# Block attention with a gated feed-forward: q and k loads of the first batch on one queue, k in whole-head pieces, and a new order of all steps

## The chip, the cores and the metric

One core of a Trainium2 chip runs the kernel. The metric is the device time of one execution in microseconds (us); less is better. The kernel before takes 654.4 us (median of 3 runs, 654.33 to 655.25).

The core's engines run side by side, each with an instruction stream of its own, and wait for one another by semaphores: TensorE (PE, matmuls; its weight loads are listed as PEld), VectorE (DVE), ScalarE (ACT), GpSimd (POOL) and SyncE (SP, which here only issues DMAs). ScalarE and GpSimd can issue DMAs too.

## The reference, cut to what matters

```python
# q, k, v: (4, 8, 768, 64); block = 32, window = 16
k_sum = k.reshape(B, H, nb, block, D).max(axis=3)      # one key per block of 32
v_sum = v.reshape(B, H, nb, block, D).mean(axis=3)     # one value per block
scores_l = where(|i - j| < window, q @ k.T / 8, -1e9)
scores_s = q @ k_sum.T / 8 + log(block)
a = softmax(concat([scores_l, scores_s]))               # with + 1e-9 under the sum
x = (a @ concat([v, v_sum])).transpose(0, 2, 1, 3).reshape(3072, 512)
h = x @ w_in                                            # 512 x 2048
g = h - tanh(h)
return g @ w_out                                        # 2048 x 512
```

All numbers are float32. The program computes its matmuls with operands split in a high and a low part, which is why names such as wh and wl, gh and gl come in pairs.

## The kernel before

The 3072 tokens are eight units u of 384 (two to a batch of 768 tokens), the eight heads two groups g of four, a unit three tiles i of 128 tokens, the 2048 columns of the feed-forward sixteen tiles f of 128. For each unit and group the kernel makes the scores of the 384 queries against 96 local and 24 block keys (`scores`), the softmax in four steps (minimum with the mask on VectorE, exp on ScalarE, the sum's inverse on VectorE, the multiplication called "normal" on any engine), the transposes of the probabilities ("p turn" on TensorE, "p out" back to SBUF), and the values (`values`, out of the tile o). Then come the two matmuls of the feed-forward: "in" (pH), the gate, and "out" (pY). The weights go through `convert`: a load of 512 KB into one of three wraw buffers, then the steps scale, shift, low, sign, which split them into their high and low parts.

q and k need a transposition before they can be used: `load_half` (L809) brings 384 tokens of four heads as four pieces of 96 KB, one for each head, and a "q turn" or "k turn", one instruction of VectorE, that transposes them once all four have landed. `top` (L826) then takes the maximum over each block of k, and "top put" copies it beside the keys. For the first half of the program's work the pieces have buffers in the tiles wg0, wg1 and wg4 (`raw_slots`, L797: six halves); all others ("lazy", L799) go through a single buffer, raw, so that the next four pieces can't be written before the turn of the last four has read it. `load_v` (L847) and `put_mean` (L858) fill the tile vw from v and from the block means with pieces that SP or GpSimd may issue.

Nothing here is issued where the code makes it. `do`, `either` and `dma` record each step as a task with the engines that can run it, what it reads and what it writes, and `Plan.follow` (L150) issues all tasks afterwards. The order of the tasks is a list of 3628 numbers written out in the source, `ORDER` (L29); `ON` (L33) has a letter for each task, which names the engine where there is a choice (P, A, D, S for GpSimd, ScalarE, VectorE, SyncE); `FILL` (L32) says ahead of which tasks TensorE runs keep-warm matmuls whose results nobody reads, and how many: long ones of 512 columns until the scores, short ones of 128 after them. Within an engine the instructions run in the order of that list; a task that waits holds up what is behind it on its engine. The planner's costs (the rates in `dma`, L463) serve for plans without a list. All instructions show the line L58, the wrapper that issues them, so rows are told apart by tile names: wg<-in_k and wg<-in_q are the first batch's q and k pieces, raw<-in_k and raw<-in_q the lazy ones, kT<-wg, qT<-raw and oo<-raw the turns, prob, stat and probT the softmax, mean the block means, vw<-in_v and vw<-mean the pieces for the values.

SP's list begins with the four v pieces of group 0, then k, q and v pieces mixed. The first seven entries of ScalarE's list are five k pieces and two q pieces of the first batch, which it issues as DMAs (`both=b == 0` in `load_half` allows that). GpSimd makes the constants (the identity, the mask, zeros), then issues seven v pieces and three mean puts.

## Time and profile before

| what | value |
|---|---|
| median of 3 runs | 654.4 us (654.33 to 655.25) |
| the profiled execution | 654.0 us |
| its span, first to last instruction | 652.3 us |
| TensorE busy | 628.0 us (96%) |
| VectorE busy | 447.1 us (69%) |
| ScalarE busy | 451.2 us (69%) |
| GpSimd busy | 163.3 us (25%) |
| moved by DMA | 113.23 MB |
| mean granted clock of TensorE | 0.996 |

The page comes from one execution. Busy time is the time in which an engine executes; DMA issues and waits are not in it. The stretches (windows) give the same by time, the waits say what an engine's idle time ended with, the chain of waits follows what ended last in a stretch back through what released it, and the timeline lists one engine's instructions. The granted clock is the share of the full speed (1.00 is 2.4 GHz) at which TensorE was allowed to run.

### The profile page before, as it was taken

What the parts mean: (1) busy time and instruction counts of PE and PEld (TensorE: products, weight loads), DVE (VectorE), ACT (ScalarE), POOL (GpSimd) and SP (SyncE); (2) the same over time, 40 slices, a digit from 0 to 9 for tenths busy, and PEclk for the clock granted to TensorE, in tenths of its full rate; (3) what the DMA queues carried; (4) which work ended last, traced back from release to release, by engine and by line L of the source; (5) the groups of instructions that cost most, each with busy time, mean ns of one, the idle gap of its engine ahead of it and who ended that gap; (6) DMA issues with size and microseconds to landing.
All of it is one profiled execution on the core that took longest, in us unless ns stands there. A gap on an engine that the chain in (4) does not pass through costs nothing.

```text
span 652.3 us, 15013 instructions
## 1 busy us (share of the span) xinstructions
PE 628.0 (96%) x5221; PEld 522.9 (80%) x5221; DVE 447.1 (69%) x1271; ACT 451.2 (69%) x1372; POOL 163.3 (25%) x263
## 2 busy tenths in 40 slices
PE   5799899999999999999999999999999999999997
PEld 2464566678888799989888899989888899999885
DVE  3899999996988774555677875645687863333563
ACT  3879798988889755547699865556589754334783
POOL 2302300124202332434533313114311221112120
PEclk9999989999999999999999999999999999999999
DMA  9777787765677586756353356656623145554101
GB/s 237 196 235 224 235 242 227 208 201 167 232 245 261 183 257 210 252 164 213 112 157 116 92 163 218 206 165 198 184 72 95 34 166 190 161 177 148 48 1 51
DMA packets 119340, 113.23 MB, mean 174 GB/s; under 512 B 43561, under 2 KB 87017, under 8 KB 119261
## 3 DMA queue, kind: packets, MB, share of 16 engines
q1 hardware_dynamic: 116716, 109.84, 54.6%
q10 hardware_dynamic: 2176, 1.87, 1.0%
q8 instruction: 42, 0.69, 0.4%
q0 software_dynamic: 368, 0.53, 0.3%
q14 instruction: 38, 0.30, 0.1%
HBM read 88.87 MB, written 20.97 MB: 168 GB/s over the span
## 4 chain that ended last, share of the span: by engine, by line
PE 72%; DMA 12%; DVE 7%; ACT 4%; SPq 2%; issue 2%; POOL 1%; DVEq 0%; ACTq 0%; POOLq 0%
PE pY L58 34%; PE pH L58 26%; PE pS L58 6%; PE pX L58 5%; SPq L58 2%; DVE tmp L58 2%; DMA wraw<-scr 2%; ACT prob L58 2%; DMA raw<-in_q_dram 2%; DMA wraw<-in_moe_w_out_dram 2%; DMA scr<-wraw 1%; DMA raw<-in_k_dram 1%; DMA tmp<-in_v_dram 1%; DVE wf L58 1%; DMA gu<-in_v_dram 1%
## 5 line engine op out<-in xcount | busy, mean ns | idle before, releaser
L58 ACT ACTIVATE prob<-prob,stat 128x120 f32<-128x120 f32 x299 | 109.0, 386 | 17.7 <-DVE stat L58 17.5
L58 PE MATMUL pY<-wl,gh 128*128 128x512 f32 x288 | 113.5, 394 | 0.0
L58 PE MATMUL pH<-wf,wraw 128*128 128x384 f32 x460 | 93.8, 339 | 0.8 <-DMA wraw<-scr 0.8
L58 PEld LDWEIGHTS pH<-wf,wraw 128*128 128x128 f32 x460 | 80.9, 188 | 4.1 <-DVE wf L58 0.9
L58 PE MATMUL pY<-wh,gh 128*128 128x512 f32 x204 | 83.1, 407 | 0.1
L58 PE MATMUL pY<-wh,gl 128*128 128x512 f32 x204 | 81.0, 397 | 0.0
L58 PE MATMUL pH<-wg,wraw 128*128 128x384 f32 x360 | 71.1, 338 | 0.0
L58 PE MATMUL pY<-wg,gh 128*128 128x512 f32 x168 | 68.6, 408 | 0.9 <-ACT gh L58 0.9
L58 ACT ACTIVATE gu<-gu 128x384 f32<-128x384 f32 x128 | 66.2, 520 | 2.1
L58 PE MATMUL pH<-o,wf 128*128 128x384 f32 x188 | 65.8, 446 | 1.6 <-DVE o L58 0.7
L58 POOL TENSOR_TENSOR gl<-gu,gh 128x384 fp32r<-128x384 f32 x32 | 34.0, 1064 | 129.4 <-ACT gh L58 77.5
L58 PE MATMUL pY<-wg,gl 128*128 128x512 f32 x168 | 66.1, 394 | 0.1
L58 PEld LDWEIGHTS pH<-wg,wraw 128*128 128x128 f32 x360 | 63.2, 188 | 3.4 <-issue 0.8
L58 PEld LDWEIGHTS pY<-wl,gh 128*128 128x128 f32 x288 | 54.4, 189 | 9.0
L58 PEld LDWEIGHTS pH<-o,wf 128*128 128x128 f32 x188 | 34.3, 190 | 17.9 <-DVE wf L58 1.5
L58 ACT ACTIVATE gv<-pH 128x384 f32<-128x384 f32 x35 | 17.2, 491 | 42.5 <-PE pH L58 42.5
L58 POOL TENSOR_TENSOR gu<-gu,gt 128x384 f32<-128x384 f32 x26 | 27.1, 1046 | 75.1 <-ACT gu L58 74.3
L58 PEld LDWEIGHTS pY<-wh,gl 128*128 128x128 f32 x204 | 38.6, 189 | 8.8 <-DVE gl L58 0.4
L58 PEld LDWEIGHTS pY<-wh,gh 128*128 128x128 f32 x204 | 38.6, 189 | 7.8 <-issue 0.6
L58 PE MATMUL pY<-wf,gh 128*128 128x512 f32 x108 | 44.8, 440 | 0.0
L58 ACT ACTIVATE gt<-gu 128x384 f32<-128x384 f32 x48 | 24.7, 518 | 22.8 <-DVE gu L58 21.2
L58 PEld LDWEIGHTS pY<-wg,gl 128*128 128x128 f32 x168 | 31.5, 188 | 7.4 <-DVE gl L58 0.5
(232 smaller groups left out, 1420.4 us busy)
## 6 DMA issues: line engine op xcount, KB each, us to landing
wraw<-scr SPq DMA_DIRECT2D x72, 512.0 KB
wraw<-in_moe_w_in_dram SPq DMA_DIRECT2D x16, 512.0 KB
wraw<-in_moe_w_out_dram SPq DMA_DIRECT2D x16, 512.0 KB
scr<-wraw SPq DMA_DIRECT2D x16, 512.0 KB
wraw<-scr SPq DMA_DIRECT2D x24, 256.0 KB
raw<-in_q_dram SPq DMA_DIRECT2D x56, 96.0 KB
vw<-in_v_dram SPq DMA_DIRECT2D x59, 80.0 KB
raw<-in_k_dram SPq DMA_DIRECT2D x48, 96.0 KB
```

The lines of the kernel that those rows point to most:

```text
L58: return lambda *args, **kwargs: self._tc.keep_in_program_order(op(*args, **kwargs))
```

## The change

It has four parts.

- `load_half` loses its `both`: no q or k piece may be issued by ScalarE. The seven pieces go to SP.
- The first batch's k is loaded by a new function, `load_whole`, once for each head group: four pieces of 192 KB, each with both halves of one head, into wg0 and wg4, and two k turns that each wait for all four. q keeps its halves, in wg1. There are eight tasks fewer.
- `ORDER`, `ON` and `FILL` are new from end to end (3620 tasks). SP begins with v, k, v, v, v, k, k, k, then the four q pieces of group 0, then the rest. GpSimd issues twelve v pieces and two mean puts, the first of them right behind its constants; the memset of the zeros beside group 1's keys stands behind ten of these, of which the fourth is a mean put. The mean put that ran on GpSimd as its seventh DMA is on SP. TensorE's list has values matmuls of unit 0 earlier among the first "in" matmuls, the p turns of unit 1, group 1 in another order with the "in" matmuls of the same unit directly behind them, and ahead of the "out" matmuls. Of the tasks with a choice VectorE has ten more than before, ScalarE eight fewer and GpSimd three fewer. FILL has three long matmuls ahead of three tasks as before, and four and three short ones where it had one, two, two and two.
- Two numbers change that have no effect on the issued program: the rate 270e3 (the planner's start times, which a list of the right length overrides), and the 36 in a branch for units listed in `OUT7`, which is empty.

```diff
-ORDER = [1, 6, 13, 14, 27, 15, 16, 117, 0, 9, 28, 30, 10, 17, 24, 19, 18, 20, 22, 29, 48, 46, 25, 47,
...
+ORDER = [15, 17, 16, 1, 9, 6, 2, 3, 10, 13, 14, 109, 4, 19, 110, 18, 20, 111, 23, 24, 25, 42, 41, 44,
...
-FILL = {125: 3, 154: 3, 190: 3, 188: 1, 215: 2, 262: 2, 286: 2}
+FILL = {117: 3, 146: 3, 182: 3, 180: 4, 278: 3}
-ON = 'PPAPAPPDDPPPPSSSSASSADASSADASAADDPSSSS
...
+ON = 'PPAPAPPDDPPPPSSSSSSSSDDSSSSDDASPSSPSPSPPP
...
-            kind, (0.04, 270e3) if run < 1024 else (0.0, 330e3))
+            kind, (0.04, 250e3) if run < 1024 else (0.0, 330e3))
...
-    raw_slots = [(tag, n) for tag in ("wg0", "wg1", "wg4") for n in range(2)]
+    raw_slots, raw_wholes = [("wg1", n) for n in range(2)], ["wg0", "wg4"]
...
-            dma(which + " load", lambda e, h=h, src=src: e.dma_start(x()[32 * h:32 * h + 32].rearrange("p j r d -> p j (r d)"), src), 32 * JH * 2 * D * 4, 2 * D * 4, w=[(base, (n, h))], both=b == 0)
+            dma(which + " load", lambda e, h=h, src=src: e.dma_start(x()[32 * h:32 * h + 32].rearrange("p j r d -> p j (r d)"), src), 32 * JH * 2 * D * 4, 2 * D * 4, w=[(base, (n, h))])
...
+    def load_whole(b, g):
+
+        to, tag = qk_base(b, g)[1], raw_wholes.pop(0)
+        base = buf(("raws", tag), tag, [P, 2, JH, 2, D])
+        for h in (0, 2, 1, 3):
+            src = k[b, HG * g + h].rearrange("(j b r) d -> b j (r d)", j=2 * JH, r=2)
+            dma("k load", lambda e, h=h, src=src: e.dma_start(at(base)[32 * h:32 * h + 32].rearrange("p a j r d -> p (a j) (r d)"), src), 64 * JH * 2 * D * 4, 2 * D * 4, w=[(base, h)])
+        for j in range(2):
+            do("k turn", DVE, TURN_COST, lambda j=j: turn("k", at(base)[:, j], at(to), j), r=[(base, h) for h in range(HG)], w=[(to, j)])
...
     for g in range(NG):
-        load_half("k", 0, g, 0, False)
+        load_whole(0, g)
         load_half("q", 0, g, 0, False)
-        load_half("k", 0, g, 1, False)
         top(0, g)
...
-            if small_only and OUT7 and j >= 36 and (j - 36) % 3 == 0 and (j - 36) // 3 < FH:
-                make_out_sums((j - 36) // 3)
+            if small_only and OUT7 and j >= 66 and (j - 66) % 3 == 0 and (j - 66) // 3 < FH:
+                make_out_sums((j - 66) // 3)
```

## Rows read from the trace of the kernel before

**Rows 1.** The page: TensorE's busy time, and GpSimd's DMA queue (packets, MB, share).

```profile
PE 628.0 (96%) x5221; PEld 522.9 (80%) x5221; DVE 447.1 (69%) x1271; ACT 451.2 (69%) x1372; POOL 163.3 (25%) x263
...
q0 software_dynamic: 368, 0.53, 0.3%
```

**Rows 2.** Stretches: time, busy us (instructions) per engine, granted clock, DMA share, GB/s.

```profile
0.00:16.00 16.00, 8.14 (x110) 4.34 (x116) 4.78 (x6) 4.76 (x20) 4.19 (x22) 1.00 0.94 234
16.00:38.00 22.00, 17.26 (x286) 11.07 (x287) 18.47 (x79) 17.97 (x74) 6.42 (x18) 1.00 0.76 200
...
72.00:88.00 16.00, 12.96 (x134) 8.78 (x133) 14.75 (x49) 13.59 (x48) 5.70 (x5) 0.89 0.86 251
88.00:131.00 43.00, 42.49 (x359) 28.77 (x358) 40.68 (x108) 39.52 (x116) 3.40 (x4) 1.00 0.74 220
...
164.00:252.00 88.00, 85.68 (x781) 73.69 (x782) 72.28 (x204) 65.37 (x196) 20.29 (x28) 1.00 0.72 238
252.00:612.00 360.00, 359.79 (x2775) 320.67 (x2774) 217.01 (x632) 228.19 (x687) 100.36 (x154) 1.00 0.49 153
```

**Rows 3.** What TensorE waited for: us in total, times, longest.

```profile
PE pS L58 <- ACT prob L58: 2.6, 3, 1.3
...
PE pH L58 <- DVE oo L58: 1.5, 1, 1.5
PE pH L58 <- POOL mask L58: 1.4, 1, 1.4
PE pS L58 <- DMA vw<-mean: 0.8, 1, 0.8
```

**Rows 4.** A shorter stretch of the same table, 83.9 to 87.3 us.

```profile
83.90:87.30 3.40, 3.40 (x10) 2.63 (x9) 2.65 (x13) 2.57 (x11) 0.00 (x0) 0.50 0.97 270
```

**Rows 5.** The chain of waits, 0 to 45 us: start, duration, what.

```profile
11.35 2.60 DMA wg<-in_q_dram
...
24.06 0.22 ACT mean L58
...
25.93 4.74 DMA vw<-mean
```

**Rows 6.** The table of stretches again, 11 to 15 us.

```profile
11.00:15.00 4.00, 3.17 (x52) 1.25 (x50) 3.78 (x5) 1.32 (x7) 0.07 (x1) 1.00 1.02 256
```

**Rows 7.** ScalarE's timeline at the start: start, duration, instruction, idle time before.

```profile
7.36 1.28 ACT L58 ACT_TABLE_LOAD   x1 [7.36 <-DMA wg<-in_k_dram]
```

**Rows 8.** GpSimd's timeline, 0 to 45 us: its first DMA issue.

```profile
16.96 0.72 POOL L58 DMA_DIRECT2D vw<-in_v_dram  x1
```

**Rows 9.** VectorE's timeline, 15 to 45 us.

```profile
21.49 0.98 DVE L58 STREAM_TRANSPOSE wg<-wg 128x768 f32<-128x768 f32 x1 [0.73 <-POOL wg L58]
...
31.68 0.56 DVE L58 COPY o<-pS 128x384 f32<-128x384 f32 x1 [0.87 <-PE pS L58]
```

**Rows 10.** The chain of waits, 40 to 92 us.

```profile
46.41 4.66 DMA raw<-in_k_dram
...
72.54 3.82 DMA wraw<-in_moe_w_in_dram
...
76.45 0.68 ACT tmp L58
77.13 1.75 ACT prob L58 x9
...
81.93 0.52 ACT wh L58
```

**Rows 11.** VectorE's timeline, 41 to 92 us.

```profile
45.43 1.25 DVE L58 CAST wh<-wf 128x512 fp32r<-128x512 f32 x1
...
53.84 0.28 DVE L58 TENSOR_SCALAR prob<-prob,stat 128x120 f32<-128x120 f32 x1
...
73.35 0.98 DVE L58 STREAM_TRANSPOSE oo<-raw 128x768 f32<-128x768 f32 x1
```

**Rows 12.** TensorE's timeline, 71 to 92 us: two waits on ScalarE's probabilities.

```profile
81.13 0.61 PE L58 MATMUL pS<-ident,prob 128*120 128x128 f32 x2 [0.25 <-ACT prob L58]
83.08 0.65 PE L58 MATMUL pS<-ident,prob 128*120 128x128 f32 x4 [1.34 <-ACT prob L58]
```

4 lines of the change are left out of this document (2 added, 2 removed).

## The prediction

> **What bounds the kernel now.** Three views, in this order: the page's busy shares, the table of stretches, and TensorE's waits; then the chain of waits in the two stretches where TensorE is not full. The page says that TensorE is busy 628.0 of 652.3 us [rows 1]: whatever else the change does, at most 24 us can be won from outside the matmuls, and the matmul count does not change. The stretches say where the 24 us lie [rows 2]: 7.9 us in the first 16 us, 4.7 in 16 to 38, 3.0 in 72 to 88, 0.5 in 88 to 131, 2.3 in 164 to 252, next to nothing in the 360 us behind that, and 4.6 at the very end (the last store, which the change doesn't reach). So the change is decided in the first 90 us, and the question behind that is how much of a gain is given back between 88 and 252 us, where VectorE is busy 40.68 of 43 us and ScalarE 39.52 [rows 2].
>
> The waits name the releasers [rows 3]: ScalarE's probabilities 2.6 us in three waits (the longest 1.3), one wait of 1.5 on VectorE's oo (the q turn ahead of the scores of unit 1, group 1), 1.4 on POOL's mask (the first scores), 0.8 on the block means that a DMA brings back. Beside the waits stands one loss that no wait shows: from 83.9 to 87.3 us the granted clock is 0.50, the lower level (1.2 of 2.4 GHz) [rows 4]; what ran in those 3.4 us would have taken 1.7 at the upper level. It follows the waits on ScalarE's probabilities.
>
> The time against which I add is the profiled run: 654.0 us, span 652.3, so 1.7 us outside the span. The median is 654.4, 0.4 above; I add 0.4 at the end.
>
> **The start (0 to 16 us).** Before the first scores the same v, k and q bytes have to land, in the old and in the new order; 8 of the k issues become 4 of double size. In the trace the last q piece lands 2.60 us after its issue, at 13.95 [rows 5]; behind it come the q turn on VectorE, the top copy and the mask on POOL, and the scores. Meanwhile the DMA engines move 256 GB/s at a mean share of 1.02 [rows 6]: the start is bound by bytes, not by issues. Five k pieces and two q pieces leave ScalarE's queue, which starts its table load only at 7.36, behind them [rows 7]; ScalarE has no other work then that anyone waits for, so I give its earlier start nothing. SP takes over those pieces, but with the double size it issues 16 k and q pieces there, where it had 17 of the 24: no more issue time than before. What I can't read is the new load of POOL's queue: 12 v pieces and two mean puts issued, by their place in the new order, from about 6 us on, where the old kernel issues its first at 16.96 [rows 8] and 10 in all, with 0.53 MB, or 53 KB each [rows 1]. At 0.72 us an issue [rows 8], at most some six of them, 0.32 MB, could be under way before the q pieces land: 0.32 MB at 256 GB/s are 1.25 us of delay. For a gain speaks that k is there in fewer pieces, that top, turn and mask no longer queue behind each other (TensorE waits 1.4 us for the mask [rows 3]). I take -0.4 us, bounds -1.2 and +1.3.
>
> The Trainium skill ("DMA: Bandwidth & Descriptors", section "Issuing engines are not separate DMA queues") says that transfers started from SP, ScalarE or GpSimd all run on the same 16 engines, so that another issuing queue saves sequencer time alone. The trace agrees as far as it goes: with two queues issuing, the share is full and the rate no higher than later with one. By that rule dropping ScalarE's queue costs nothing, as taken above. The same page ("Queues, rings and completion order") says that an engine serves its queue rows in turn, packet by packet; no run here shows it yet, and it speaks against this change: POOL's early pieces would then not wait behind SP's. That is the third rival.
>
> **16 to 45 us.** The mean put that released the first values matmuls was issued by POOL at 25.93 and landed 4.74 us later [rows 5]; it now stands on SP with 5.67 instead of 5.93 MB of transfers ahead of it (counted in the two orders), some 1 us sooner (gain up to the 0.8 of its wait). VectorE's stall of 0.73 us on a memset of POOL [rows 9] moves: the memset now stands behind ten of POOL's issues, of which the fourth waits for a block mean (about 12 us, as on SP before), so at 12 + 7 x 0.72 = 17 us, still ahead of its reader. Against that, VectorE gets 1.4 us more to do ahead of the turn that starts the lazy q and k loads (softmax normals that ScalarE and POOL had, two block means), and loses the 0.56 us copy of o that it took at 31.68 [rows 9]. The keep-warm matmuls are nine long and seven short in both; the short ones move to where TensorE waits anyway, and cost nothing as long as the wait behind them is longer than the 0.9 us of four. I take -0.3, bounds -1.6 and +1.4.
>
> **The raw chain (45 to 74 us).** The lazy pieces of q and k share one buffer, so each set of four waits for the turn of the set before: the first k set lands 4.66 us after its last issue at 46.41 [rows 10]. Ahead of the first k pieces a weight load waited for VectorE; in the new order three of four k pieces stand before that load, and the weight step it waits for comes about 1 us sooner behind the turn. Over the whole stretch up to the last q turn (73.35 [rows 11]), VectorE loses the copy of o (0.56), one cast of 1.25, and five normals of 0.28, and gets seven normals and two block means of about 0.22 (ScalarE's time for the same step [rows 5]; VectorE has no such row, bounds 0.1 and 0.4); the other moves (a probT copy, a weight scale) cancel. Net 1.25 + 0.56 - 2 x 0.28 - 2 x 0.22 = 0.8 us less [rows 11]. So the turn comes at about 71 to 72, TensorE arrives 0.7 us earlier, and of its wait of 1.5 us I take 1.2 away; bounds -1.5 and +0.8 (the turn 1.4 later by VectorE's extra work in front, without the gain on the load).
>
> **The softmax behind it (76 to 88 us).** Old: a weight step of 0.68 whose load landed at 76.36 stands ahead of nine exps on ScalarE, and a cast of 0.52 (81.93) between the normals that release the transposes [rows 10]. New: that weight load is issued about 3 us sooner, the five normals on ScalarE stand together and a sixth is VectorE's, so the transposes come 0.6 + 0.7 us sooner. TensorE's waits there are 0.25 + 1.34 us [rows 12]; I take 1.2 away, bounds -1.6 and 0. With no such wait ahead of it I expect the granted clock to stay: -1.4 of the 1.7, bounds -1.7 and 0.
>
> **What is late next.** The sum so far is -0.4 - 0.3 - 1.2 - 1.2 - 1.4 = -4.5 us. TensorE then reaches 88 us 4.5 us sooner, but VectorE was busy 14.75 of the 16 us before and has only 2.3 us free in 88 to 131 [rows 2], and in the new assignment it has 1.5 us more to do up to about 165 and still 1.4 more up to 236, while ScalarE has some 3 us less. Part of what TensorE gains it will wait for VectorE. From below nothing (TensorE's work there is unchanged, its waits 0.5 us), from above 4.4, where VectorE paces it throughout; I take +1.7, nearer to the row of 88 to 131, in which TensorE hardly waits. Behind 252 us TensorE is full and nothing moves.
>
> Sum: 652.3 - 4.5 + 1.7 = 649.5 of span, 651.2 with the 1.7 outside, 651.6 against the median: I say 651.5.
>
> **Rivals.**
> 1. VectorE becomes the bound in 88 to 252 us: the same gains, and 4.0 to 4.4 of them given back. 654.4 - 4.5 + 4.2 = 654.1. For it: 95% busy there [rows 2] and ten more tasks; against it: TensorE's waits in that stretch name VectorE for little of the old 2.3 us.
> 2. The gains in the start and the raw chain come, but the softmax behind the scores ends no sooner, since nine exps and the normals are ScalarE's whatever stands between: 1.2 + 1.4 stay lost, and little is given back (+0.7). 654.4 - 1.9 + 0.7 = 653.2, a faster time within 0.2% of the old.
> 3. Slower: POOL's early v pieces take their share from SP's k and q. It decides from the point where the first q turn starts later than 14.8 + 0.4. Price: 1.25 us at the first scores, which everything behind inherits, and the raw chain starts 1.4 us later by VectorE's extra work ahead of it, so the wait at 73 us grows by 0.8 and the low clock stays; 654.4 + 1.25 + 0.8 = 656.5. For it: the share of 1.02 [rows 6]; against it: the fourth of those issues waits for a mean, so perhaps only three (0.16 MB, 0.6 us) come before the q pieces.
> 4. That the change does not do what it says (k in larger pieces, and no ScalarE issue, moving nothing, the rest of the order a draw): 654.4, a case within the first rival's band.
>
> **How the numbers follow.** About 0.2% (1.3 us) is what a measurement of this kernel can tell from no change. Forecast 0.5 (648.5 to 653.0), rival 1 with 4 0.22, rival 2 0.13, rival 3 0.15. Faster by over 1.3 us: the forecast and most of rival 2's lower edge, 0.57; within: rivals 1, 4, and the rest of 2, 0.25; slower: rival 3 and a little for low clocks that I can't place, 0.18. The range: 648.5 at the low end (the terms at -6.0 and nothing lost more), 656.5 at the high end, at rival 3's price, so that about 0.12 is left out.
>
> **What would show it.** Right: no ScalarE issue before its table load, which starts near 1 us; first scores at 15 to 16 us; the q turn at 71 to 72 and no wait of TensorE over 0.5 us there; transposes without the 1.34 us wait, and a granted clock of 1.00 throughout 72 to 98. Wrong: first scores later than 16.5; a new wait of TensorE on VectorE (wf, probT, gl) in 88 to 252; a second stretch at the 0.50 clock; POOL's issues still the last to land before the first values.

## The result: slower, and the profile after

The changed kernel takes 657.85 us (median of ten runs, 655.32 to 660.37), the kernel before 652.83 beside it (ten runs, 649.99 to 655.25): a ratio of 1.0078 [1.0052, 1.0103]. Run again in a later series it gave 1.0090 [1.0066, 1.0114]. So it is slower by 5 to 6 us, where 651.5 and a gain were predicted, and it lies above the range.

The two profiled executions don't show these 5 us. The changed kernel's took 655.73 us (span 654.0) and is among its fastest; that of before took 654.0 and is among its slower ones. They differ by 1.7 us, and single executions of one kernel differ by up to 5. So the traces are read for what happens, and sizes are taken from repeated runs.

The page of after: TensorE's busy time, which answers [rows 1], and GpSimd's queue.

```profile
PE 627.5 (96%) x5221; PEld 522.1 (80%) x5221; DVE 448.8 (69%) x1281; ACT 448.9 (69%) x1369; POOL 168.2 (26%) x260
...
q0 software_dynamic: 544, 0.79, 0.5%
```

The stretches of after, with the columns of [rows 2]; the last two are the stretch of [rows 4] and a new one.

```profile
0.00:16.00 16.00, 8.29 (x120) 4.40 (x127) 4.86 (x6) 5.19 (x19) 9.12 (x34) 1.00 0.95 221
16.00:38.00 22.00, 18.75 (x286) 10.93 (x270) 19.81 (x82) 16.83 (x71) 3.21 (x8) 0.92 0.84 209
38.00:72.00 34.00, 31.62 (x325) 18.70 (x323) 31.94 (x79) 27.77 (x85) 6.92 (x8) 1.00 0.78 230
72.00:88.00 16.00, 13.60 (x136) 8.31 (x137) 15.45 (x47) 13.87 (x47) 4.42 (x5) 1.00 0.82 243
...
252.00:612.00 360.00, 359.17 (x2773) 319.99 (x2772) 213.64 (x632) 223.96 (x680) 108.62 (x153) 1.00 0.50 153
...
24.20:27.40 3.20, 3.20 (x6) 1.39 (x5) 3.20 (x8) 3.15 (x14) 0.65 (x1) 0.50 0.63 147
83.90:87.30 3.40, 2.81 (x11) 1.80 (x11) 3.32 (x17) 2.80 (x10) 0.00 (x0) 1.00 0.90 255
```

The lower clock has left the place where it stood, 83.9 to 87.3 us, and there is a stretch of 0.50 at 24.2 to 27.4 instead; the last section of the experiments shows that both come and go between executions. What TensorE waited for in after (us in total, times, longest), beside [rows 3]:

```profile
PE pS L58 <- DVE prob L58: 2.1, 1, 2.1
PE pH L58 <- DVE oo L58: 1.6, 1, 1.6
...
PE pH L58 <- DVE qT L58: 1.4, 1, 1.4
...
PE pS L58 <- ACT prob L58: 0.9, 1, 0.9
```

The waits on ScalarE's prob have fallen from 2.6 to 0.9 us. The first scores no longer wait for the mask, but just as long, 1.4 us, for the q turn (qT; in before 0.5). The wait on oo has grown by 0.1 where it should have shrunk by 1.2, and one of 2.1 on VectorE's prob is new. It ends at 22.2 us, and the clock falls behind it. TensorE's timeline of before, 17 to 31 us (start, duration, instruction, idle time before it and what ended it):

```profile
21.30 0.90 PE L58 MATMUL pS<-ident,prob 128*120 128x128 f32 x4 [1.03 <-ACT prob L58]
23.03 0.41 PE L58 MATMUL pS<-ident,prob 128*120 128x128 f32 x2 [0.84 <-ACT probT L58]
23.28 2.74 PE L58 MATMUL pY<-ident 128*128 128x512 f32 x6
```

The same three of after:

```profile
22.20 0.93 PE L58 MATMUL pS<-ident,prob 128*120 128x128 f32 x4 [2.09 <-DVE prob L58]
23.88 0.57 PE L58 MATMUL pS<-ident,prob 128*120 128x128 f32 x2 [0.75 <-DVE stat L58]
24.24 4.34 PE L58 MATMUL pY<-ident 128*128 128x512 f32 x6
```

Six long keep-warm matmuls take 4.34 us instead of 2.74. Part of the delay of prob goes back to VectorE's timeline of after, 14 to 18 us, where the minima with the mask stand behind the second q turn:

```profile
14.35 0.99 DVE L58 STREAM_TRANSPOSE qT<-wg 128x768 f32<-128x768 f32 x1
17.04 0.98 DVE L58 STREAM_TRANSPOSE oo<-wg 128x768 f32<-128x768 f32 x1 [1.70 <-DMA wg<-in_q_dram]
```

The first q turn starts at 14.35 (before 14.79), the second at 17.04, after 1.70 us in which VectorE waited for its last q piece; in before it started at 15.68, right behind the first. The four pieces for it were issued from 10.84 us in after and from 10.25 in before: the issue is 0.6 later, the turn 1.4. The pieces ahead of these do not stand as the section on the change has them: by the trace SP issues three q pieces, three v pieces, the fourth q piece at 9.48 us and one more v piece before them.

The first of the minima in before, where VectorE had been waiting for the scores:

```profile
17.59 0.28 DVE L58 CUSTOM_DVE_ANT_0 prob<-pH,mask 128x120 f32<-128x120 f32 x1 [0.97 <-PE pS L58]
```

and in after, with the weight step behind them:

```profile
18.05 0.28 DVE L58 CUSTOM_DVE_ANT_0 prob<-pH,mask 128x120 f32<-128x120 f32 x1
...
19.65 0.43 DVE L58 TENSOR_SCALAR tmp<-wraw 128x512 f32<-128x512 f32 x1 [0.30 <-DMA wraw<-in_moe_w_in_dram]
```

The p turn comes 0.90 us later than in before (22.20 for 21.30). The late q turn accounts for 0.46 of that. VectorE also waits 0.30 us for a weight load, and it has a copy of a block mean (0.22 us at 21.61) ahead of the normals, which are its own now.

The end is longer, too. The last matmul starts at 647.42 us in before and at 647.31 in after: TensorE was no later, although the span is 1.7 us longer. The 1.7 us of this pair of traces lie wholly behind the last matmul.

### The profile page after: what moved, and what is told of

Read it like the earlier page. It is cut to its first block, busy times and chain, and to the rows that moved or that the text cites. A ratio compares the mean times of both kernels' runs of the same rounds, so it can differ in the third digit from the quotient of the medians.

```text
span 654.0 us, 15007 instructions
## 1 busy us (share of the span) xinstructions
PE 627.5 (96%) x5221; PEld 522.1 (80%) x5221; DVE 448.8 (69%) x1281; ACT 448.9 (69%) x1369; POOL 168.2 (26%) x260
## 4 chain that ended last, share of the span: by engine, by line
PE 73%; DMA 10%; DVE 9%; issue 2%; SPq 2%; ACT 2%; POOL 1%; DVEq 0%; ACTq 0%; POOLq 0%
PE pY L58 34%; PE pH L58 28%; PE pS L58 6%; PE pX L58 5%; DVE wraw L58 2%; DVE tmp L58 2%; SPq L58 2%; DMA wg<-in_q_dram 2%; DMA wraw<-in_moe_w_out_dram 2%; DMA wraw<-scr 2%; DMA wraw<-in_moe_w_in_dram 1%; DMA wg<-in_k_dram 1%; DMA scr<-wraw 1%; DMA raw<-in_k_dram 1%; DMA raw<-in_q_dram 1%
## 5 line engine op out<-in xcount | busy, mean ns | idle before, releaser
L58 ACT ACTIVATE prob<-prob,stat 128x120 f32<-128x120 f32 x304 | 111.8, 386 | 38.7 <-DVE stat L58 38.3
L58 POOL TENSOR_TENSOR gl<-gu,gh 128x384 fp32r<-128x384 f32 x27 | 29.2, 1082 | 135.6 <-ACT gh L58 110.4
L58 POOL TENSOR_TENSOR gu<-gu,gt 128x384 f32<-128x384 f32 x34 | 35.5, 1046 | 79.8 <-ACT gu L58 68.5
L58 ACT ACTIVATE gh<-gu 128x384 fp32r<-128x384 f32 x47 | 24.3, 517 | 23.3 <-PE pY L58 17.6
L58 ACT ACTIVATION_READ_ACCUMULATOR prob<-prob,stat 128x1 f32 x192 | 36.4, 190 | 0.0
```

What stands on the lines that cost most here:

```text
L58: return lambda *args, **kwargs: self._tc.keep_in_program_order(op(*args, **kwargs))
```

## Experiments

Each kernel below was timed in five rounds beside the kernel before, the changed kernel itself among them. Ratios to it, with their 95% intervals:

| kernel | order | k pieces of the first batch | who issues them | median us | ratio |
|---|---|---|---|---|---|
| after_again | new | 192 KB | SP | 657.58 | 1.0090 [1.0066, 1.0114] |
| before_whole | old | 192 KB | SP | 655.56 | 1.0064 [1.0046, 1.0083] |
| before_sp | old | 96 KB | SP | 652.70 | 1.0009 [0.9992, 1.0026] |
| before_whole_act | old | 192 KB | SP and ScalarE | 651.11 | 0.9989 [0.9977, 1.0001] |
| before_whole_alt | old | 192 KB, halves alternate | SP | 650.98 | 0.9987 [0.9969, 1.0004] |
| before_sp_runs | old | 96 KB, halves in runs | SP | 653.44 | 1.0024 [1.0004, 1.0044] |
| after_halves | new | 96 KB | SP | 654.66 | 1.0052 [1.0034, 1.0069] |
| after_halves_act | new | 96 KB | SP and ScalarE | 653.18 | 1.0024 [1.0008, 1.0040] |
| after_halves_act_pool | new | 96 KB | SP and ScalarE | 652.87 | 1.0018 [1.0000, 1.0036] |
| after_whole_act | new | 192 KB | SP and ScalarE | 653.97 | 1.0033 [1.0017, 1.0049] |
| after_start_alt | new | 192 KB, halves alternate | SP | 656.80 | 1.0068 [1.0043, 1.0093] |
| after_pool_late | new | 192 KB | SP, with ten v pieces | 656.31 | 1.0073 [1.0052, 1.0095] |
| after_pool_late_alt | new | 192 KB, halves alternate | SP, with ten v pieces | 655.96 | 1.0053 [1.0031, 1.0074] |
| mixed | old, new from 72 to 90 us | 192 KB, halves alternate | SP | 653.90 | 1.0029 [1.0011, 1.0047] |
| best_try | old but for two steps | 192 KB, halves alternate | SP | 653.36 | 1.0033 [1.0017, 1.0049] |

("Halves" are partitions 0 to 63 and 64 to 127 of the buffer: a piece fills one quarter of the partitions.)

> The changed kernel once more. In the two traces at hand TensorE ends its last matmul at 647.6 us (changed) and 647.7 (before), yet the spans are 654.0 and 652.3: by these traces all of the difference lies behind the last matmul. Theory 1 (the end): the ratio to before is 1.0025, that is 1.7 us, in every run. Theory 2 (the clock): the number of stretches at the granted clock of 0.50 differs from run to run, the runs spread over some 5 us, and the ratio is 1.005 to 1.010 with a mean clock below that of before.

### The two parts apart: the pieces and the queue without the new order

before_whole has the source of the changed kernel and the order of the kernel before.

```diff
-ORDER, ON, FILL of after
+ORDER, ON, FILL of before; each pair of 96 KB pieces of k becomes the 192 KB piece, all k and q pieces on SP
```

> The kernel before with the named part of the change alone: the first batch's k in four pieces for each head group (192 KB each), and all q and k pieces on SP; the order of everything else is the old one. Theory A (the start is bound by bytes, as predicted): within 0.5 us of before. Theory B (the issues count): SP issues what ScalarE issued beside it, so that the first scores come 1 to 2 us later and the time is 1 to 2 us longer. Theory C (the new order is what costs): before_whole is like before, and the changed kernel is slower than both.

Measured 1.0064, about 4 us slower. The part that the change is named after costs most of the loss, without any new order. (Its profiled execution, 653.43 us, is the lowest of its runs, so the 4 us can't be looked for there.) Three kernels split it: the queue alone (before_sp), the size alone (before_whole_act).

```diff
 before_sp: the kernel before, but
-ON = '... A' for five k and two q pieces of the first batch
+ON = '... S' for them
 before_whole_act: before_whole, but
-k load, q load: SP alone
+k load, q load: both=True, and two k and two q pieces of group 0 have 'A' in ON
```

> The kernel before with one thing changed: the five k and two q pieces that ScalarE's queue issued go to SP, at their place in the order; pieces and order are the old ones. The named part as a whole (pieces and queue, run as before_whole) cost 4 us. Theory Q (the queue: SP alone issues too slowly, 24 pieces of 96 KB behind each other): 655 to 656 us, 3 to 4 us above before. Theory S (the size of the pieces): within 1 us of before.

> The kernel before with k in four pieces of 192 KB for each head group, and ScalarE's queue kept for two of them and for the two q pieces that it had. Theory S (the size of the pieces, and both k turns waiting for all four): 655 to 656 us, as before_whole. Theory Q (the queue): within 1 us of before, 652 to 653.

Neither costs anything that can be measured (1.0009 and 0.9989). So in the old order neither the lost second queue nor the large piece costs anything by itself; the two together do. What is special about the two together is in SP's list: with nothing from ScalarE between them, K h0, q h0, q h1, K h1 follow each other, 576 KB that all go to partitions 0 to 63. before_whole_alt changes nothing but that sequence.

```diff
-SP: v v v v K0 q0 q1 K1 K2 K3 v v q3 v q2 v ...
+SP: v v v v K0 K2 q0 K3 K1 q3 v v q1 v q2 v ...
```

(K a 192 KB piece of k, q a piece of q; the number is the quarter of the partitions it fills.)

> before_whole with the same pieces on the same queue, only in another order among themselves: pieces for partitions 0 to 63 (heads 0 and 1) and pieces for 64 to 127 (heads 2 and 3) alternate, where before_whole issues four of the first kind (576 KB) and then two of the second behind one another. Theory P (a queue that fills one half of the partitions for a while moves less per microsecond): 652 to 653 us, 3 us less than before_whole, and over 245 GB/s in 4 to 12 us where before_whole has 207 to 225. Theory Z (the size alone, or both turns' waiting for all four pieces): 655 to 656, as before_whole.

Measured 0.9987: the whole loss is gone, 4.6 us for a permutation of SP's first pieces. The times of before_whole lie in two groups, 653.4 to 654.2 and 657.0 to 657.3, so the size is rough; but its lowest, 653.43, is above the highest of before_whole_alt, 653.40. The stretches show what changed. 4 to 12 us in before_whole:

```profile
4.00:12.00 8.00, 5.45 (x51) 3.03 (x51) 0.00 (x0) 2.98 (x16) 0.47 (x4) 1.00 1.13 216
```

and in before_whole_alt:

```profile
4.00:12.00 8.00, 5.93 (x52) 3.21 (x52) 1.49 (x2) 2.99 (x16) 0.49 (x4) 1.00 1.09 260
```

The DMA engines are just as busy (1.13 and 1.09) and move 216 instead of 260 GB/s: a full share isn't a full rate. The second q turn starts at 17.53 us with the one list and at 15.68 with the other. Each rate is that of one execution. The changed kernel itself has 251 GB/s in this stretch, and three more executions with its start 234 to 259, against 268 in before and 259 in before_last_store_sp: with the new order the rate is only a little lower.

before_sp_runs asks whether the sequence alone is enough, with the small pieces: the same 576 KB for one half in a row, in six pieces.

```diff
 before_sp, SP's first pieces of k and q (quarters):
-0 2 3 0 q1 1 2 3 q0 1 q3 q2 ...
+0 0 1 1 q0 q1 2 2 3 3 q2 q3 ...
```

> The counterpart: before_sp (small pieces, all on SP) with its pieces sorted, those for partitions 0 to 63 first and then those for 64 to 127, for each head group. Theory P: 655 to 656 us, like before_whole, and 200 to 225 GB/s in 4 to 12 us. Theory Z: 652.7, as before_sp.

Measured 1.0024, 0.7 us over before_sp, with 249 GB/s in 4 to 12 us against 247. So the sorting costs little with 96 KB pieces. Shown is that the rate depends on the sequence when the pieces are of 192 KB; that the halves of the partitions are the reason fits both alternating kernels, but why small pieces suffer less isn't settled. Nor is it shown how a rate that is lower for 8 us comes to cost 4.6 us at the end of the program.

### The new order without the named part

```diff
 after_halves: the source of before (96 KB pieces), all on SP, in the new order
-raw_slots = [(tag, n) for tag in ("wg0", "wg1", "wg4") for n in range(2)]
+raw_slots = [("wg0", 0), ("wg1", 0), ("wg0", 1), ("wg4", 0), ("wg1", 1), ("wg4", 1)]
 after_halves_act: the same, and ScalarE's list begins with its seven pieces, as in before
```

> The changed kernel with k in the old pieces (96 KB, each turn behind its own four), all issued by SP at the place of the large ones; the order is the new one. Theory S: 4 us less than the changed kernel, about 653.5 (1.9 of the new end stay). Theory Q: as the changed kernel or slower, 657 to 659, since SP has eight issues more.

> The new order alone: k in the old pieces, and the same five k and two q pieces on ScalarE's queue as before, ahead of its other work; everything else as in the changed kernel. By both S and Q the named part is undone, and what is left is the new order: before plus the 1.9 us that the new order's end is longer, 653.5 to 654, if the order is otherwise even. If it comes out at 657 or more, the order itself costs, not the named part.

Without ScalarE's queue the new order is at 1.0052; large pieces (after_again) add 2.9 us to that, of which 1.9 lie at the end (below). With both queues the new order alone is 1.0024 [1.0008, 1.0040], some 1.2 to 1.6 us slower, where the prediction's sum had the whole change 2.8 us faster. Its gain in the raw chain is real for most of the way, as long as the named part is left out: the lazy turns start at 41.05, 50.19, 56.07, 62.16 and 67.69 us in after_halves_act, against 41.63, 51.51, 57.41, 62.66 and 68.69 in before (42.83, 51.81, 58.12, 63.30 and 68.74 in the changed kernel). Then it is lost in one step: the last q turn starts at 74.25 (before 73.35 [rows 11]). VectorE's timeline of after, 70 to 76 us, has the same step:

```profile
70.66 0.69 DVE L58 SCALAR_TENSOR_TENSOR tmp<-wraw,tmp 128x512 uint32<-128x512 uint32 x1
71.27 1.76 DVE L58 TENSOR_TENSOR wf<-wf,wh 128x512 fp32r<-128x512 f32 x1
72.96 1.48 DVE L58 SCALAR_TENSOR_TENSOR wf<-wraw,tmp 128x512 uint32<-128x512 uint32 x1
...
75.30 0.97 DVE L58 STREAM_TRANSPOSE oo<-raw 128x768 f32<-128x768 f32 x1
```

and GpSimd's timeline of after in the same time:

```profile
71.03 1.45 POOL L58 TENSOR_TENSOR wl<-tmp,wh 128x512 fp32r<-128x512 f32 x1 [4.51 <-ACT wh L58]
72.45 1.45 POOL L58 TENSOR_TENSOR gu<-gu,gt 128x384 f32<-128x384 f32 x1
```

Two steps of VectorE that take 0.68 and 0.68 us in before last 1.76 and 1.48, exactly while GpSimd runs two operations with two tensors each; those take 1.45 each, 1.27 and about 1.0 in before. In before GpSimd began at 72.98, when VectorE was done with such steps. The Trainium skill has this ("SBUF — State Buffer", section "Who interferes with whom"): an instruction of VectorE with two inputs in SBUF and one of GpSimd that reads SBUF contend for a shared read port; the trace agrees, 0.68 against 1.76 us. The trace of before had such a meeting as well, at 65 us:

```profile
64.67 1.54 POOL L58 TENSOR_TENSOR gh<-gu,gt 128x384 f32<-128x384 f32 x1 [1.54 <-ACT gt L58]
65.25 1.51 DVE L58 TENSOR_TENSOR wf<-wf,wh 128x512 fp32r<-128x512 f32 x1
```

The same step of VectorE takes 1.51 us there, so the price could have been read before the change was run. The next kernel takes the cause away.

```diff
 after_halves_act, but 'w low part' 0 (wl) and 'g' 4 (gu):
-on GpSimd, beside VectorE's weight steps
+on VectorE, right behind the last q turn
```

> after_halves_act (the new order alone) with two steps of GpSimd (a low part of a weight, wl, and one product of the gate, gu) given to VectorE right behind the last q turn. In its trace they run at 69.99 (1.45 us) and 71.40 (1.44 us), beside two steps of VectorE of 1.76 and 1.48 us that take 0.68 elsewhere, and ahead of the q turn at 74.25. Theory L (the two engines hold each other up, and that is why the turn is 1.9 us later than the order would have it): the two steps take 0.7 us, the turn comes at 72.2 to 72.6, TensorE's wait of 1.9 us ahead of these scores shrinks to under 0.5, and the time falls by 1 to 2 us, to 651.2 to 652.2. If VectorE's steps stay long, or the wait is taken over by the values and o steps ahead of the turn, no change: 653.2.

VectorE's timeline of after_halves_act_pool, 69 to 74 us:

```profile
69.72 0.69 DVE L58 TENSOR_TENSOR wf<-wf,wh 128x512 fp32r<-128x512 f32 x1
70.32 0.69 DVE L58 SCALAR_TENSOR_TENSOR wf<-wraw,tmp 128x512 uint32<-128x512 uint32 x1
...
72.93 0.98 DVE L58 STREAM_TRANSPOSE oo<-raw 128x768 f32<-128x768 f32 x1 [0.99 <-DMA raw<-in_q_dram]
```

The mechanism is shown: both steps are back at 0.69. The time isn't won: the turn now waits 0.99 us for its q piece, so it gains 1.3 of the 1.9, TensorE's wait there falls from 1.89 to 1.26, and behind it the lower clock returns (0.61 in 83 to 87 us). The kernel takes 652.87 us, 0.3 less than without, which can't be told from nothing.

### The softmax step, and the two orders joined

The prediction put -1.2 and -1.4 us on the softmax at 76 to 88 us. mixed runs before_whole_alt up to the scores there, the new order's next 210 tasks, and the old order again. best_try makes in before_whole_alt the two moves of ScalarE alone that the prediction named.

```diff
 mixed: order of before_whole_alt up to 'scores' 3; new order and engines up to 'scores' 4; then before_whole_alt
 best_try: before_whole_alt, but on ScalarE
-'w scale' 13 ahead of nine exps; 'w high part' 1 between the normals
+'w scale' 13 behind four of them; 'w high part' 1 behind the six normals
```

> before_whole_alt up to the scores of unit 1, group 1 (73 us), then the new order for the next 210 steps, up to the first scores of unit 2, then the old order again. In the traces the new order lost less between 76 and 131 us (1.3 us in after_halves_act, against 3.8 in before) and more behind it (131 to 300 us: 4.6 against 3.0). Theory: the new order's softmax behind those scores keeps its gain, and its later losses are left out: 1 to 2 us less than before_whole_alt, 649 to 650. Rival: what the new order gained there was only taken from the waits behind, and VectorE hands it back: 651, as before_whole_alt.

> before_whole_alt with two steps of ScalarE moved: the scale of weight 13 behind four of the exps of unit 1, group 1, instead of ahead of all, and the high part of a weight behind the six normals instead of among them, as the new order has it. It tests that step of the prediction by itself, in the old order. Theory: the transposes come 0.6 to 1.2 us sooner, TensorE's wait of 1.34 us at 81.75 shrinks to under 0.6, and the time falls by 0.5 to 2 us below before_whole_alt, to 649 to 650.5. Rival (VectorE, or the weights behind those steps, take the gain back): 651, as before_whole_alt.

Both were slower than before_whole_alt (653.90 and 653.36 against 650.98). In mixed the waits are short, as predicted (0.37 and 0.75 us; before has 0.25 and 1.34, before_whole_alt one of 1.34), and the clock stays at 1.00, as it does in before_whole_alt. So there was little to win, and TensorE loses 5.1 us in 88 to 252 us, where before_whole_alt loses 3.0 and the old order at most 4.3. In best_try the wait only changes its cause. TensorE's timeline of best_try, 74 to 92 us:

```profile
81.50 0.61 PE L58 MATMUL pS<-ident,prob 128*120 128x128 f32 x2 [1.28 <-ACT prob L58]
83.55 0.86 PE L58 MATMUL pS<-ident,prob 128*120 128x128 f32 x4 [1.44 <-DVE probT L58]
```

What became of the softmax is in VectorE's and ScalarE's timelines of best_try, 73 to 86 us:

```profile
78.22 0.43 DVE L58 TENSOR_SCALAR tmp<-tmp 128x512 uint32<-128x512 uint32 x1 [1.50 <-ACT tmp L58]
...
81.05 1.82 ACT L58 ACTIVATE prob<-prob,stat 128x120 f32<-128x120 f32 x6 [0.78 <-DVE stat L58]
```

VectorE now waits 1.50 us for the scale that was moved behind the exps, and makes the sum's inverse (stat) only behind its own weight steps. So ScalarE's normals begin at 81.05 us, where they begin at 79.36 in before_whole_alt.

### What the named part costs in the new order

After_halves_act to after is a step of 4.4 us by the medians. Putting ScalarE's queue back, alternating the halves, and taking GpSimd's early v pieces away (the third rival's cause) were tried.

```diff
 after_whole_act: after with two k and two q pieces of group 0 at the head of ScalarE's list
 after_start_alt: after with SP's sequence of before_whole_alt
 after_pool_late: after, but ten v pieces
-on GpSimd, from 5.8 us on
+on SP, behind the k pieces of group 1
 after_pool_late_alt: after_pool_late with SP's sequence of before_whole_alt
```

> The changed kernel with two of its large k pieces and two q pieces issued by ScalarE, first in its list, as in before_whole_act. It completes the table of order, size and queue. If size and one queue cost only together, as they did in the old order: 4 us less than the changed kernel, 653 to 654. If in the new order the size costs by itself: 656 to 657. The end of 6.7 us behind the last matmul, where the others have 4.9, stays if it belongs to the new order with the large pieces.

> The changed kernel with only its first twenty SP loads (and the four large k pieces of group 1) in the sequence of before_whole_alt: the four v pieces first, then pieces for partitions 0 to 63 and for 64 to 127 in turns. Theory P (the sequence of pieces on the one queue is what the named part cost): 655 to 656 us, 2 us less than the changed kernel, and the second q turn near 15.7 us instead of 17.0. If the start is not what costs in the new order: 657 to 658. The end of 6.7 us behind the last matmul stays.

> The changed kernel with the ten early v pieces of GpSimd's queue (0.5 MB at the old 53 KB each, issued from 5.82 us on) given to SP, behind the last large k piece of group 1. Theory R (the third rival of the prediction: GpSimd's pieces take their share of the engines while SP's q pieces wait): the second q turn comes at 15.6 to 16.2 us instead of 17.0 to 18.1, and the time falls by 1.5 to 2 us, to 655.6 to 656.1. If SP's own sequence is what delays it: no change there, 657.6 or more, since SP has ten issues more.

> Both: GpSimd's early pieces on SP behind the k pieces, and SP's first pieces in the sequence of before_whole_alt. Theory R together with P: the start is that of before_whole_alt, the second q turn at 15.7, and the time is that of the new order alone plus the longer end: 653.2 + 1.9 = 655.1, or less. If the start of the new order is not what the named part costs: 656.5 to 657.5.

The second queue takes 3.6 us back (653.97). Alternating alone takes 0.8, which can't be told from nothing, and the second q turn doesn't come sooner (17.78 us). Taking the v pieces off alone doesn't move it either (17.13). Both together do. VectorE's timeline of after_pool_late_alt, 10 to 18 us:

```profile
14.26 0.97 DVE L58 STREAM_TRANSPOSE qT<-wg 128x768 f32<-128x768 f32 x1
15.90 0.98 DVE L58 STREAM_TRANSPOSE oo<-wg 128x768 f32<-128x768 f32 x1 [0.67 <-DMA wg<-in_q_dram]
```

So with large pieces on SP the late turn has two causes, each enough by itself in these executions, one of each kernel: the run of pieces for one half, and GpSimd's early v pieces. That is the third rival's mechanism, at the second q turn and not at the first. With small pieces and both queues GpSimd's early v pieces do no such harm: in after_halves_act the second turn follows the first at 16.18 us without a wait. That the late turn costs time is not shown. The kernel with both causes removed still takes 655.96 us, with the ten v pieces in SP's list and the first lazy turn at 44.64 instead of 42.83; its wait on VectorE's prob is still 1.86 us, with one of 0.68 for the weight load ahead of it; and after_whole_act takes 653.97 us although its second turn starts at 17.93.

### The end

Three kernels ask why 6.7 us lie behind the start of the last matmul in after and 4.9 in before: the last store on the other queue, in both orders, and a longer list of TensorE (two more keep-warm matmuls).

```diff
 after_last_store_act:  y store 23 in ON  S -> A
 before_last_store_sp:  y store 23 in ON  A -> S
 after_pad:  FILL = {117: 3, 146: 3, 182: 3, 180: 4 -> 6, 278: 3}
```

> The changed kernel with one letter of ON put back: the first half of the last result tile is stored by ScalarE's queue, as before, not by SP behind two others. Theory 1 (the end): 1.3 to 1.7 us shorter than the changed kernel once more, last matmul to end 4.6 us instead of 6.4. Theory 2 (the clock): no difference beyond the spread.

> The kernel before with the same one letter changed: the first half of the last result tile is stored by SP. Theory 1 (the end): 1.3 to 1.7 us longer than before (ratio 1.002 to 1.003). Theory 2: within 0.1% of before.

> The changed kernel with two more short keep-warm matmuls (six instead of four ahead of the values of unit 0), which make TensorE's list as long as before and shift nothing else. Theory C (the longer end hangs on where the instructions lie in memory: the profile shows one more packet on an instruction queue there): the end behind the last matmul is 4.9 us again, and the time 1.5 to 2 us less, 655.7 to 656.3. If the end belongs to the order itself: 6.7 us and 657.6, as the changed kernel.

The queue isn't it: the end is 6.8 us with ScalarE's queue in the new order (1.0106 [1.0083, 1.0128] for the kernel) and 4.9 with SP's in the old (1.0012 [0.9994, 1.0030]). The length of TensorE's list isn't it: 6.75 us in after_pad (1.0075 [1.0050, 1.0101]). Every kernel with the new order, large pieces and no ScalarE issue has the long end unless its v pieces were moved (4.75 and 4.7 us); with ScalarE's issues back (after_whole_act) it is 6.1, with four packets of the instruction queue and not five; all with small pieces, and all with the old order, have 4.8 or 4.9. The DMA view of before, 645 to 660 us: the rate in 40 slices, then the instruction queue (packets, MB, share):

```profile
GB/s 0 0 0 0 0 208 431 60 0 371 374 380 273 44 87 0 0 0 0 0 0 0 0 0 0 0 0 0 0 0 0 0 0 0 0 0 0 0 0 0
...
q14 instruction: 4, 0.03, 0.8%
```

The same of after:

```profile
GB/s 0 0 0 0 0 333 361 6 93 388 382 372 164 109 22 0 0 0 0 0 0 0 0 22 0 0 0 0 0 0 0 0 0 0 0 0 0 0 0 0
...
q14 instruction: 5, 0.04, 1.0%
```

The stores are done at the same time, and some 3 us later one more packet of the instruction queue moves, just ahead of the end. As after_whole_act shows, it doesn't go with every long end. What fetches it, and why its coming depends on the start of the program, was not found. About 1.9 us of the loss are shown to lie here, without a cause.

### Where the new order loses, over all executions

One execution of each kernel lets TensorE's loss (length of the stretch less busy time multiplied by the granted clock) be averaged: old order (before, before_last_store_sp, before_whole, before_sp, before_whole_act, before_whole_alt, before_sp_runs), the changed kernel (after, after_again, after_last_store_act) and the new order with small pieces (after_halves, after_halves_act, after_halves_act_pool).

| us lost by TensorE | 0 to 16 | 16 to 38 | 38 to 72 | 72 to 88 | 88 to 252 | 252 to 612 |
|---|---|---|---|---|---|---|
| old order, 7 executions | 7.6 | 5.2 | 0.9 | 3.2 | 3.6 | 0.3 |
| changed kernel, 3 | 8.6 | 4.8 | 1.7 | 2.5 | 3.7 | 1.0 |
| new order, small pieces, 3 | 8.6 | 3.8 | 1.4 | 3.7 | 3.1 | 1.4 |

The spread within a group is up to 3 us in a column (16 to 38: 3.46 to 6.15 for the changed kernel; 88 to 252: 2.78 to 4.30 for the old order), so only what repeats counts: about 1 us more at the start (not in the profiled pair: 7.9 in before, 7.7 in after), 0.5 to 0.8 in 38 to 72, and 0.7 to 1.1 in 252 to 612 (0.83 or more in every one of the six, at most 0.76 in the seven).

The changed kernel's loss against the old order is 1.4 us by this table, and 1.9 at the end. The mean granted clock differs as well: 0.9943 over the timed runs of after_again, 0.9975 over those of before beside it, and 0.0032 of 652 us are 2.1 us. But 1.4 of these are in the table already, as the profiled executions had 0.9957 and 0.9979 in the mean, and from run to run the time hardly follows the clock: after took 659.45 us at 0.996 and 655.32 at 0.994. With at most 0.7 left for the clock, 1 to 2 of the 5 to 6 us are not accounted for. The two groups with the new order lose nearly the same, 22.2 and 22.0 us in all, so of the 4.4 us that the named part costs there only the 1.9 at the end are located. Nor does the table show the 4 us of before_whole (it loses 20.4 us in all, the seven 20.8 in the mean).

The stretches at the lower level move from run to run: 24.2 to 27.4 us in after, but in after_again, the same program,

```profile
22.80:29.40 6.60, 5.85 (x10) 2.16 (x9) 6.46 (x22) 5.35 (x22) 0.90 (x2) 0.51 0.62 150
```

and none in after_last_store_act, which has the same start, a second q turn at 17.82 us and a wait of 1.55 on prob:

```profile
16.00:38.00 22.00, 18.54 (x330) 11.44 (x330) 19.37 (x82) 16.75 (x71) 3.23 (x8) 1.00 0.86 214
```

before_whole_alt, whose second q turn is not late, has one there:

```profile
24.20:27.40 3.20, 3.20 (x12) 0.87 (x10) 3.17 (x8) 3.13 (x14) 1.89 (x3) 0.62 0.47 101
```

Between 16 and 38 us three of the four executions with the changed kernel's start have a stretch at the lower level (after, after_again and after_pad), and two of the seven with the old order. It may come more often with the change; but the table has no more loss there, 4.8 us against 5.2. And the stretch at 83.9 to 87.3 us [rows 4] is in the profiled execution of before alone: the six others with the old order have 1.00 from 72 to 88 us, before_whole_alt with the same wait of 1.34.

## Why the prediction was wrong, point by point

The timed runs split the loss in two. With the named part left out, the new order gains nothing: 1.2 to 1.6 us slower (after_halves_act). The named part, all q and k pieces on one queue and k in large pieces, costs 4.4 us more in the new order (653.18 to 657.58) and some 4 in the old (1.0064). The prediction had -0.4 for it, with +1.3 as the upper bound. That is the step that failed first.

- **What bounds the kernel.** Right: TensorE's busy time is unchanged (627.5 for 628.0 us), and all that differs lies in the first 90 us, the end, and small waits between. "The last store, which the change doesn't reach" was wrong: the end is 1.9 us longer.
- **The start, -0.4.** The forecast rows came: ScalarE loads its table at 0.88 us, and the first scores start at 15.73 (before 15.90). The wait on the mask went, but one just as long, on the q turn, took its place. The step that failed is that the queue and the piece size were put at nothing, the queue's move costed by counting issues and the rest by "bound by bytes, not by issues" from [rows 6]. That took 256 GB/s at a full share for the rate of any sequence, and before_whole has 216 at a full share. Either part alone is worth nothing in the old order, as reckoned; what was not asked is what SP's list looks like with both. There the 4.6 us go with the halves alternating. In the new order alternating doesn't bring them back, and how the 4.4 us arise there, beyond the 1.9 at the end, stays open. The prediction also ended the start at the first scores. The pieces behind them, for the second q turn, it partly misread: the piece that lands at 13.95 [rows 5] was issued at 10.98 and is one of these four, where the last for the first scores is issued at 9.28. In the changed kernel that turn is 1.4 us later. TensorE's two waits at 22 to 24 us are 2.84 us instead of 1.87, of which the turn explains 0.46, and the low clock of 24.2 to 27.4 costs 1.6 more in this execution and nothing in another.
- **16 to 45, -0.3.** In the profiled pair the loss of 16 to 38 us is the same (4.7). The mean put on SP is a real gain, as reckoned: before waited 0.83 us for it at 30.7 us, after doesn't wait at all. In this pair the wait on prob takes that gain back.
- **The raw chain, -1.2.** The working of VectorE's load was right up to 68 us in after_halves_act (turns 0.5 to 1.3 us sooner). In the changed kernel the turns are 0.05 to 1.2 us later than in before, as the chain starts later, and the conclusion is wrong in both: the last turn is at 74.25 and 75.30 instead of 71 to 72. The step that failed is that durations were carried over from the old trace as they stood: 0.68 us for a step of VectorE beside an idle GpSimd became 1.76 beside a busy one. The engine to which a step moves was looked at, the one that runs beside it was not. Two new waits, 0.90 on ScalarE's prob at 53.6 and 0.63 on gh at 59.6, weren't foreseen.
- **The softmax, -1.2 and -1.4.** The waits came as forecast in the new order: the two of 0.25 and 1.34 [rows 12] are one of 0.75, now on ScalarE's probT. The granted clock at 83.9 to 87.3 is 1.00, but that is luck of the execution: the low clock there was the one profiled run's, and in six of seven executions with the old order there was nothing to win. TensorE's loss of 72 to 88 us fell from 4.5 to 2.4 in this pair, from 3.2 to 2.5 in the means. And it is a property of the whole list and not of the two moves named: best_try, with these alone, has waits of 1.28 and 1.44.
- **What is late next, +1.7.** Not tested: the term rested on TensorE reaching 88 us 4.5 us sooner, and by the table the changed kernel has lost 17.6 us up to there, the old order 16.9. In 88 to 252 us it loses 3.7 and the old order 3.6, so VectorE's fuller list costs nothing that can be seen here; what it would cost a kernel that arrives sooner, rival 1's question, stays open. mixed, where the two orders meet, loses 2.1 more there than before_whole_alt. "Behind 252 us nothing moves" was wrong by 0.7.
- **Rival 3** was right in its sign. Its mechanism was seen (after_pool_late_alt), at the second q turn instead of the first, where its own condition, a first turn later than 15.2 us, wasn't met. That it costs time isn't shown: with the v pieces moved the kernel has 1.0073 against 1.0090, and the intervals overlap. Its price, 656.5, came from 1.25 us of transfers and a low clock that stays; the end and the run of pieces for one half were not in it, so that it comes near to the measured time is luck.
- **The range** held no term for a cost at the end, none for a lower rate, and took a low clock that belongs to one execution as the kernel's own.

What stays open: the 1.9 us at the end, 1 to 2 us that no trace accounts for, why the size of the pieces matters for the rate, and what the late second q turn and GpSimd's v pieces cost in the new order. No version was shown to beat the kernel before: before_whole_alt has 0.9987 [0.9969, 1.0004].

## What to carry to other kernels

Where one queue issues the first loads in large pieces, try letting those for partitions 0 to 63 and 64 to 127 alternate: here it was worth 4.6 us in one order of the steps, nothing clear of noise in the other, and little with 96 KB pieces. Two parts of a change that cost nothing each can cost much together, so time them together. Follow the last piece that each consumer needs, and not the first matmul only. A duration holds for what ran beside it: when a step of VectorE with two inputs moves, look at what GpSimd does at that time. A stretch at the lower clock in one trace may not be there in the next execution. Half a per cent can't be read from one trace of each kernel: here the two profiled executions were 1.7 us apart and the medians 5.

## What the runs showed of the hardware

- The same bytes in another sequence on one queue move at 216 or 260 GB/s while the DMA engines are busy all the time, 192 KB pieces of 32 partitions each, one execution of either. The Trainium skill ("SBUF — State Buffer", section "Door 1: The DMA port swizzle (why `[64,N]` ≈ `[32,N]`)") says that partitions 0 to 63 and 64 to 127 are reached by different ports, eight each. These two rates agree with that; the 249 GB/s of before_sp_runs, with 96 KB pieces in runs, don't.
- A VectorE step of 0.68 us takes 1.76 beside one of GpSimd that reads two tensors (1.51 at 65 us in before), and GpSimd's slows from 1.27 to 1.45 as well.
- The end of the program took 4.9 or 6.7 us behind the start of the last matmul with the same stores at the same time.
- The same program has the lower clock for 3.2 us in one execution (after) and for 6.6 in another (after_again).
